# Attention with global and local tokens, then a gated feed-forward layer: the staging of the first two batches rearranged

## The chip, the cores and the metric

The kernel runs on one core of a Trainium2 chip. A core has five engines that each run their own instructions in order: TensorE (PE in the profile: matrix products; PEld its weight loads), VectorE (DVE), ScalarE (ACT), GpSimd (POOL) and SyncE (SP), which here only issues DMAs. They wait for one another through semaphores. Sixteen DMA engines move data between device memory and the on-chip memory (SBUF); TensorE writes only to PSUM, from which VectorE or ScalarE must copy.

The metric is device time in microseconds, the median over several runs of the same program.

## The reference

Eight batches, eight heads, 512 local and 32 global tokens, head width 64. Global queries see all 544 keys; a local query sees the 32 global keys and the local keys within 32 positions. The result goes through a feed-forward layer.

```python
k_all = np.concatenate([k_g, k_l], axis=2)
v_all = np.concatenate([v_g, v_l], axis=2)
out_g = np.matmul(sm(scale * q_g @ k_all.T), v_all)
s_ll = np.where(np.abs(pos[:, None] - pos[None, :]) <= 32, scale * q_l @ k_l.T, -1e9)
s_lg = scale * q_l @ k_g.T
a_l = sm(np.concatenate([s_lg, s_ll], axis=-1))
out_l = np.matmul(a_l, np.concatenate([v_g, v_l], axis=2))
...
h = x @ w_in                       # x: 4352 x 512, w_in: 512 x 2048
g = h * np.clip(h + 3.0, 0.0, 6.0) / 6.0
return (g @ w_out).astype(np.float32)
```

(The transposes are written short.)

## The kernel before

Work is cut into 32 pairs `p` of two heads; a batch `b` has `NM` = 4 pairs. A local pair takes these steps, each a helper:

- `load(p, what)` (L117) issues on SP the DMA of k, q or v, 256 KB of float32 each, into one of 16 staging tiles `stg`. `cast` (L131) makes float16 of it: on GpSimd, but for pair 0's k and q, which VectorE takes. `vshift` (L142) copies half of v into `vb`, whose rows 64 to 95 hold the 32 global values.
- `emit_Tp` (L238) transposes k and q on TensorE; `copy_k` (L249, VectorE) and `copy_q` (L256, ScalarE or VectorE) bring them to SBUF. `emit_T` (L262) does all three and a fourth, small copy at L267: the last 32 queries are repeated in front of the others. For the first four pairs this copy is not made; `emit_Ss` (L313) splits the first window's product in two instead (L319, `p < NM`).
- `emit_S(p, ch)` (L345) and `emit_S4(p)` (L337) compute scores: two matmuls of 512 columns per half `ch` put a mask into PSUM (L310), small matmuls add q times k (L326), ScalarE takes the exponential (L335). Each half has 128 keys; the second holds the 32 global keys beside its local ones.
- `emit_AV(p)` (L370) multiplies by `vt` and `vb` and divides (VectorE, L390 and L391). `emit_X(p)` (L433) transposes the result and copies it to `xt` (VectorE, or ScalarE with `True`).

The global keys go through `load_g`, `cast_G`, `emit_Gp`, `copy_G` (L180 to L213) into `kgT`, and `kglob` or `kglob_m` (L220, L233) repeats them four times in the key tile. The global values are fetched by `load_vg` (L154), a DMA on GpSimd's queue that also casts, and `vglob_m` (L226, VectorE) or `vglob` (L146, GpSimd, later batches) repeats them four times into `vb`. `vgsum` (L151) copies them to `vgs` for the global queries.

The feed-forward layer is cut into units that are put between the steps of attention. `u1(c)` (L467) multiplies four blocks of `w_in` by the four `xt` of the batch into one PSUM tile, 16 values of `c` per batch; ScalarE (L477) and VectorE (L479) make `gt` of it. `u2(t, c4)` (L484) multiplies four `gt` by four blocks of `w_out`. `load_w` and `cast_w` (L159, L168) bring in sixteen blocks of `w_in` and sixteen of `w_out`; `u1(c)` needs blocks 4*(c//4) to 4*(c//4)+3.

The order of every engine is written out by hand: first all loads of batches 0 and 1, the weights and pair 8 (L532 to L563, SP's order), then GpSimd's casts in the same order (L618 to L650), then the steps of TensorE, VectorE and ScalarE (L655 on). The first two batches (pairs 0 to 7) transpose on TensorE; later ones by DMA. From `emit_SG(0)` (L732), the first scores of the global queries, the text of the program is the same in both versions. SP's and ScalarE's DMAs share eight completion semaphores in turn: each DMA waits, in its issuing queue, for the one that had its semaphore before it.

Of the kernel before, what the change touches and what calls it, by code (L numbers as in the profile page):

```python
# [14 lines left out]
def kernel(  # L15
# [12 lines left out]
    nc = tc.nc  # L28
# [4 lines left out]
    dm, dff = moe_w_in.shape  # L33
    NM = H // 2
    NC = dff // P
    NT = Sl // P
# [21 lines left out]
    def const(name, shape, dtype=FP16):  # L58
        return constp.tile(shape, dtype, tag=name, name=name)
# [11 lines left out]
    kgT = const("kgT", [P, NM, B, Sg])  # L71
    vg = const("vg", [P, B, H, D])
    kTs = [const(f"kT{i}", [P, NM, NT * KW + W]) for i in range(2)]
# [4 lines left out]

    NRUN = 2
    NE = 4  # L80
# [65 lines left out]
    def vglob(b, eng):  # L146
        eng.tensor_copy(out=vbs[b % NV][rg, :, :, vc],
                        in_=vg[rg, b].rearrange("s (m h) d -> s m (h d)", h=2).unsqueeze(1)
                        .to_broadcast([Sg, NT, NM, P]))

    def vgsum(b, eng):  # L151
        eng.tensor_copy(out=vgs[b % NV][rg], in_=vg[rg, b])

    def load_vg(b):  # L154
        nc.gpsimd.dma_start(out=vg[rg, b], in_=v_g[b].rearrange("h s d -> s h d"))

# [31 lines left out]
    def cast_G(b0, b1, nm, eng=nc.vector):  # L188
        n = wrk.tile([P, 4 * P], FP16, tag="gn", name=nm + "n", bufs=2)
        nb = b1 - b0  # L190
        eng.tensor_copy(out=n[:, 0:nb * P], in_=gst[b0, nm][:, 0:nb * P])
        gst[b0, nm, "n"] = n
# [12 lines left out]

    def copy_G(b0, b1, nm, x):
        nb = b1 - b0
        kv = (gst[b0, nm, "ps"][x * D:(x + 1) * D, 0:nb * P]
              .rearrange("p (b m e s) -> p e b m s", b=nb, m=MH, e=2))
        for e in range(2):  # L210
            r, ms = slice(e * D, (e + 1) * D), slice(x * MH, (x + 1) * MH)
            o = kgT[r, ms, b0:b1] if nm == "kg" else qgz[r, ms, b0:b1, e]
            nc.vector.tensor_copy(out=o.rearrange("p m b s -> p b m s"), in_=kv[:, e])  # L213

# [10 lines left out]

    def vglob_m(b, ms):  # L226
        n = ms.stop - ms.start
        nc.vector.tensor_copy(
            out=vbs[b % NV][rg, :, ms, vc],
            in_=vg[rg, b].rearrange("s (m h) d -> s m (h d)", h=2)[:, ms].unsqueeze(1)  # L230
            .to_broadcast([Sg, NT, n, P]))

# [29 lines left out]
    def emit_T(p):  # L262
        emit_Tp(p)
        copy_k(p)
        copy_q(p)
        s = st[p]
        nc.scalar.copy(out=s["qT"][:, 0:W].rearrange("p (i j) -> p i j", j=NT),  # L267
                       in_=s["psq"].rearrange("p (j i) -> p i j", j=NT)[:, P - W // NT:P])

# [43 lines left out]
    def emit_Ss(p, ch, exps=True):  # L313
# [4 lines left out]
        for w in range(NT):  # L318
            c0 = w * KW if ch == 0 else ((w - 1) % NT) * KW + D  # L319
            parts = [(w * P, w * P, P)]  # L320
            if w == 0 and p < NM:
                parts = [(0, Sl, W), (W, W, P - W)]
            for o, i, n in parts:
                for e in range(2):
                    r = slice(e * D, (e + 1) * D)
                    nc.tensor.matmul(out=pss[e][:, o:o + n], lhsT=kT[r, c0:c0 + P],  # L326
                                     rhs=qT[r, i:i + n], start=False, stop=True,
                                     skip_group_check=True)
# [16 lines left out]
    def emit_S(p, ch):  # L345
        emit_Sm(p, ch)
        emit_Ss(p, ch)
# [174 lines left out]
    def local_dests(b):  # L522
# [7 lines left out]
        return d  # L530

    load(0, "kq")  # L532
    load(1, "kq")
    load_g(0, 1, "kg")
    load(2, "kq")
    load(0, "v")
    load(3, "kq")
    for p in range(1, NM):
        load(p, "v")
    for i in range(4):  # L540
        load_w("in", i)
    load_g(1, 4, "kg")
    load(4, "kq")
    for i in range(4, 8):
        load_w("in", i)
    load(5, "kq")
    load(4, "v")
    for i in range(8, 12):
        load_w("in", i)
    load(6, "kq")  # L550
    load(5, "v")
    load(7, "kq")
    for i in range(12, NC):
        load_w("in", i)
    load(6, "v")
    load(7, "v")
    load_g(0, 4, "qg")
    for i in range(8):
# [17 lines left out]
    make_identity(nc, ident)  # L576
    load_vg(0)
    mb = const("mb", [P, 2, P])
# [26 lines left out]
    nc.vector.memset(vbs[0], 0.0)  # L605
    ones_v(0, nc.vector)
    mv = mneg.rearrange("p c (w q) -> p c w q", w=NT)
    nc.vector.tensor_copy(out=mv, in_=mb.unsqueeze(2).to_broadcast([P, 2, NT, P]))
# [3 lines left out]
    cast(0, "q", nc.vector)  # L612

    def first(p, what="kqv"):
        cast(p, what, nc.gpsimd)
        vshift(p, nc.gpsimd)

    cast(1, "kq", nc.gpsimd)  # L618
    cast(2, "kq", nc.gpsimd)
    first(0, "v")  # L620
    cast(3, "kq", nc.gpsimd)
    for p in range(1, NM):
        first(p, "v")
    for i in range(4):
        cast_w("in", i, nc.gpsimd)
    cast(4, "kq", nc.gpsimd)
    load_vg(1)
    for i in range(4, 8):
        cast_w("in", i, nc.gpsimd)
    cast(5, "kq", nc.gpsimd)  # L630
    first(4, "v")
    ones_v(1, nc.gpsimd)
    for i in range(8, 12):
        cast_w("in", i, nc.gpsimd)
    cast(6, "kq", nc.gpsimd)
    first(5, "v")
    cast(7, "kq", nc.gpsimd)
    for i in range(12, NC):
        cast_w("in", i, nc.gpsimd)
    first(6, "v")  # L640
    first(7, "v")
    vgsum(0, nc.gpsimd)
    fill_vg(1, nc.gpsimd)
# [9 lines left out]
    lo, hi = slice(0, NM // 2), slice(NM // 2, NM)  # L653
    HEAD = 3
    emit_Tp(0)  # L655
    copy_k(0)
    copy_q(0)
    emit_S(0, 0)
    warm_up(3)
    emit_Tp(1)  # L660
    copy_k(1)
    copy_q(1)
    emit_S(1, 0)
    emit_Gp(0, 1, "kg")
# [8 lines left out]
    emit_S(1, 1)  # L673
    vglob_m(0, lo)
    emit_S(2, 0)
    emit_AV(0)
    vglob_m(0, hi)
    emit_Tp(3)
    copy_k(3)
    copy_q(3)  # L680
    emit_S(2, 1)
    emit_X(0)
    emit_S(3, 0)
    emit_AV(1)
    emit_S(3, 1)
    emit_AV(2)
    emit_X(1)
    emit_X(2, True)
    emit_AV(3)
    for c in range(HEAD):  # L690
        u1(c, range(2))
    emit_X(3)
    for c in range(HEAD):
        u1(c, range(2, 3))
    cast_G(1, 4, "kg")
    for c in range(HEAD):
        u1(c, range(3, 4))
    emit_G(1, 4, "kg")
    u1(3)
    kglob(1, nc.vector)  # L700
    emit_T(4)
    u1(4)
    emit_S4(4)
    emit_T(5)
    vglob_m(1, lo)
    vglob_m(1, hi)
    u1(5)
    emit_S4(5)
    u1(6)
    emit_AV(4)  # L710
    emit_T(6)
    u1(7)
    emit_S4(6)
    emit_X(4)
    emit_AV(5)
    u1(8)
    emit_T(7)
    u1(9)
    emit_S4(7)
    emit_X(5)  # L720
    emit_AV(6)
    for t in Egs:
        nc.vector.memset(t[:, NT], 0.0)
    cast_G(0, 4, "qg")
    u1(10)
    u1(11)
    emit_AV(7)
    emit_X(6)
    emit_G(0, 4, "qg")
    u1(12)  # L730
    u1(13)
    emit_SG(0)  # L732
# [163 lines left out]
```

The softmax here doesn't subtract the row's maximum and nothing guards it: scores larger than these inputs give would overflow.

## Time and profile before

| | us |
|---|---|
| median of 6 runs | 317.72 |
| lowest, highest | 317.27, 318.46 |
| the profiled execution, whole | 317.7 |
| its span in the profile | 315.9 |
| TensorE busy (matmul) | 305.0 |
| VectorE, ScalarE, GpSimd busy | 211.8, 200.3, 153.8 |
| granted TensorE clock, every slice | full |

The profiled execution takes 317.7 us, of which the profile spans 315.9; the 1.8 us between them lie outside what it records. In all views times run from the span's start. A line of the timeline is: start, length, engine, source line, operation, output and input, count, and in brackets the idle time before it and what ended that idle time. A line of the chain of waits is: start, length, what. A matmul's busy time is modelled from its issue to its end; matmuls overlap, so a busy TensorE may still have gaps in its issue. The steady rate is read from rows such as "psH L472 x4" at 0.86 us in the chain: 0.215 us for 512 columns.

### The profile page before, as it was taken

The page shows a single profiled execution, that of the slowest core. Times are in us where ns is not written, and L with a number is a line of the kernel's source. Part 1 is how long each engine was busy: PE and PEld are TensorE (multiplying, and loading weights), DVE is VectorE, ACT ScalarE, POOL GpSimd, SP SyncE. Part 2 cuts the span into 40 slices and gives each one's busy share as a digit, 9 for nine tenths or more (in the row PEclk, how much of TensorE's full clock was granted, in tenths as well). Part 3 has the DMA queues.
Part 4 walks back from the last instruction along what each step waited for, and adds up shares of the span by engine and source line. Part 5 has one row for each costly group of instructions (what it writes and reads, how often), then busy time and mean ns, then how long its engine had stood idle before and what let it go on. Part 6 is the DMA issues. An engine that isn't in the chain of part 4 may idle for free.

```text
span 315.9 us, 7343 instructions
## 1 busy us (share of the span) xinstructions
PE 305.0 (97%) x2688; PEld 162.6 (51%) x2688; DVE 211.8 (67%) x484; ACT 200.3 (63%) x417; POOL 153.8 (49%) x273
## 2 busy tenths in 40 slices
PE   8887899999999999999999999999999999999995
PEld 5453555545555454555555555555555544448444
DVE  5769688896555899579945996468944962489101
ACT  6757877887444994479844994589556941579000
POOL 4777986599856675764674558543411000000000
PEclk9999999999999999999999999999999999999999
DMA  7999999999999999999999899995642002100131
GB/s 208 247 285 326 308 311 246 250 178 226 211 193 249 191 185 189 174 238 189 191 160 172 195 179 204 202 198 107 125 105 86 17 19 83 66 2 1 36 99 66
DMA packets 140260, 53.05 MB, mean 168 GB/s; under 512 B 127552, under 2 KB 131904, under 8 KB 140224
## 3 DMA queue, kind: packets, MB, share of 16 engines
q1 hardware_dynamic: 138048, 52.32, 75.6%
q0 software_dynamic: 2176, 0.26, 2.2%
q8 instruction: 21, 0.34, 0.5%
q14 instruction: 15, 0.12, 0.2%
HBM read 35.13 MB, written 8.91 MB: 139 GB/s over the span
## 4 chain that ended last, share of the span: by engine, by line
PE 79%; DVE 8%; ACT 6%; issue 3%; DMA 2%; SPq 0%; POOL 0%; ACTq 0%
PE po L488 35%; PE psH L472 30%; PE psS L297 3%; DVE gt L479 3%; ACT E L301 2%; PE pav L383 2%; PE pav L386 2%; DVE xn L391 2%; ACT t L477 2%; DMA stg<-in_q_l_dram 2%; PE psSG L357 1%; PE psS L326 1%; ACT E L335 1%; PE po L500 1%; PE pg L423 1%
## 5 line engine op out<-in xcount | busy, mean ns | idle before, releaser
L488 PE MATMUL po<-wout,gt 128*128 128x512 f16 x528 | 122.6, 379 | 0.0
L472 PE MATMUL psH<-xt,win 128*128 128x512 f16 x512 | 119.8, 379 | 2.3 <-DVE gt L479 1.2
L479 DVE SCALAR_TENSOR_TENSOR gt<-t,psH 128x512 f16<-128x512 f32 (+1 forms) x144 | 90.2, 652 | 20.3 <-ACT t L477 19.3
L477 ACT ACTIVATE t<-psH,half_col 128x512 f32<-128x512 f32 (+1 forms) x144 | 92.0, 670 | 18.0 <-PE psH L472 16.5
L472 PEld LDWEIGHTS <-win 128*128 128x128 f16 x576 | 53.3, 98 | 53.8 <-POOL win L174 2.0
L488 PEld LDWEIGHTS <-gt 128*128 128x128 f16 x528 | 48.5, 98 | 52.1
L304 DVE TENSOR_TENSOR E<-E,mk 128x512 f16<-128x512 f16 x96 | 48.1, 533 | 31.5 <-ACT E L301 30.0
L301 ACT ACTIVATE E<-psS 128x512 f16<-128x512 f32 x96 | 49.8, 604 | 13.7 <-PE psS L297 13.6
L492 ACT COPY ot<-po 128x512 f32<-128x512 f32 x16 | 9.4, 586 | 58.7 <-PE po L488 53.1
L140 POOL CAST kn<-stg 128x512 f16<-128x512 f32 x31 | 20.2, 650 | 34.8 <-DMA stg<-in_k_l_dram 34.2
L409 POOL TENSOR_TENSOR s<-Eg 128x128 f32<-128x128 f16 x24 | 10.9, 456 | 33.5 <-ACT Eg L358 32.3
L391 DVE TENSOR_TENSOR xn<-pav,rc 128x256 f16<-128x256 f32 x64 | 26.1, 422 | 1.3
L140 POOL CAST qn<-stg 128x512 f16<-128x512 f32 x31 | 20.4, 657 | 12.2 <-DMA stg<-in_q_l_dram 11.5
L492 DVE COPY ot<-po 128x512 f32<-128x512 f32 x17 | 11.7, 691 | 21.4 <-PE po L488 21.3
L140 POOL CAST vt<-stg 128x512 f16<-128x512 f32 x32 | 20.6, 644 | 8.4 <-DMA stg<-in_v_l_dram 7.8
L144 POOL COPY vb<-vt 64x512 f16<-64x512 f16 x32 | 20.4, 636 | 2.1
L383 PE MATMUL pav<-vt,E 128*128 128x65 f16 x256 | 20.1, 194 | 0.0
L335 ACT ACTIVATE E<-psS 128x512 f16<-128x512 f32 x32 | 16.9, 600 | 4.9 <-PE psS L326 4.9
L386 PE MATMUL pav<-vb,E 128*128 128x65 f16 x256 | 19.9, 195 | 0.0
L383 PEld LDWEIGHTS <-E 128*128 128x128 f16 x256 | 17.9, 99 | 3.4
L386 PEld LDWEIGHTS <-E 128*128 128x128 f16 x256 | 16.8, 97 | 3.2
L297 PEld LDWEIGHTS <-kT 64*128 64x128 f16 x384 | 10.8, 94 | 9.7 <-issue 8.0
(93 smaller groups left out, 276.7 us busy)
## 6 DMA issues: line engine op xcount, KB each, us to landing
stg<-in_k_l_dram SPq DMA_DIRECT2D x32, 256.0 KB, 3.4
stg<-in_q_l_dram SPq DMA_DIRECT2D x32, 256.0 KB, 4.2
stg<-in_v_l_dram SPq DMA_DIRECT2D x32, 256.0 KB, 4.6
out_dram<-ot SPq DMA_DIRECT2D x23, 256.0 KB, 3.7
stg<-in_moe_w_in_dram SPq DMA_DIRECT2D x16, 256.0 KB, 5.9
stg<-in_moe_w_out_dram SPq DMA_DIRECT2D x16, 256.0 KB, 4.6
out_dram<-ot SPq DMA_DIRECT2D x8, 192.0 KB, 3.8
out_dram<-ot SPq DMA_DIRECT2D x16, 64.0 KB, 2.3
```

The costliest lines, as they stand in the source:

```text
L140: eng.tensor_copy(out=o, in_=s[c + "f"])
L144: eng.tensor_copy(out=vbs[b % NV][0:D, :, m, vc], in_=vts[b % NV][D:P, :, m, vc])
L301: nc.scalar.activation(out=E[:, ch, e], in_=pss[2 * ch + e], func=EXP, scale=qk_scale)
L304: nc.vector.tensor_tensor(out=E[:, ch, e], in0=E[:, ch, e], in1=mk[:, ch].rearrange("p w c -> p (w c)"), op=mult)
L383: nc.tensor.matmul(out=o, lhsT=E[:, 0, e, w * P:(w + 1) * P], rhs=vt[:, w, m, c], start=True, stop=False, skip_group_check=True)
L386: nc.tensor.matmul(out=o, lhsT=E[:, 1, e, w * P:(w + 1) * P], rhs=vb[:, (w - 1) % NT, m, c], start=False, stop=True, skip_group_check=True)
L391: nc.vector.tensor_tensor(out=xn[:, 2 * w2:2 * w2 + 2].rearrange("p w (e d) -> p w e d", e=2), in0=po[:, :, 1:1 + P].rearrange("p w (e d) ...
L472: nc.tensor.matmul(out=ps[:, 0:n], lhsT=w_in_t[m][:, c * P:(c + 1) * P], rhs=rhs(m), start=(m == 0), stop=(m == NM - 1), skip_group_check= ...
L477: nc.scalar.activation(out=t1[:, 0:n], in_=ps[:, 0:n], func=RELU, bias=half_col, scale=1.0 / 6.0)
L479: nc.vector.scalar_tensor_tensor(out=gts[c][:, 0:n], in0=t1[:, 0:n], scalar=1.0, in1=ps[:, 0:n], op0=amin, op1=mult)
L488: nc.tensor.matmul(out=po[t][:, 0:dm], lhsT=gts[c][:, t * P:(t + 1) * P], rhs=w_out_t[c // 4][:, c % 4], start=(c == 0), stop=(c == NC - 1))
L492: (nc.scalar.copy if t % 2 else nc.vector.tensor_copy)(out=ot, in_=po[t][:, 0:dm])
```

## The change

Only the part before `emit_SG(0)` changes, and what it loads.

- Global values of batches 0 and 1: no longer fetched by GpSimd's casting DMA and repeated by four VectorE copies. SP loads them as float32 into a staging tile (`load_vgf`), GpSimd casts them into a new tile `vgp` that already holds the ones (`cast_vg`; two new fills on VectorE), and one DMA on ScalarE's queue per batch writes the four repeats (`vglob_dma`).
- Global keys of batches 1 to 3: cast, copied out of PSUM and repeated on ScalarE instead of VectorE (`copy_G(..., nc.scalar.copy)`, `kglob_a`). The cast of the global queries goes from VectorE to GpSimd.
- The small copy at L267 goes for pairs 4 to 7; their first window is split as for pairs 0 to 3.
- Loads and casts: k and q are separate entries; `w_in` blocks stand singly between the k, q and v of later pairs.
- Order of the steps: shown below. `copy_q(3)` moves to VectorE, the copy of `emit_X(1)` to ScalarE, four fills of `Eg` and four of ones to the start of VectorE's list.

```diff
-    NRUN = 2
+    vgp = [const(f"vgp{i}", [P, NM, 2 * DV]) for i in range(NRUN)]
...
-            if w == 0 and p < NM:
+            if w == 0 and p < NRUN * NM:
...
+    def kglob_a(b):
+        kv = kTs[b % 2][:, :, 0:NT * KW].rearrange("p m (u c) -> p m u c", u=NT)
+        nc.scalar.copy(out=kv[:, :, :, P:KW],
+                       in_=kgT[:, :, b].unsqueeze(2).to_broadcast([P, NM, NT, Sg]))
...
+    def load_vgf(b):
+        vgf[b] = stage()[rg].rearrange("s (h d) -> s h d", h=H)
+        nc.sync.dma_start(out=vgf[b], in_=v_g[b].rearrange("h s d -> s h d"))
+
     load(0, "kq")
     load(1, "kq")
     load_g(0, 1, "kg")
-    load(2, "kq")
+    load_vgf(0)
+    load(2, "k")
+    load(2, "q")
     load(0, "v")
...
+    load(1, "v")
+    load_w("in", 0)
+    load(2, "v")
     load_g(1, 4, "kg")
+    load_w("in", 1)
+    load(3, "v")
+    load_w("in", 2)
+    load(4, "k")
+    load_w("in", 3)
+    load(4, "q")
+    load_vgf(1)
+    load_w("in", 4)
...
+    load(7, "k")
+    load_w("in", 12)
+    load(7, "q")
+    load_w("in", 13)
+    load_g(0, 4, "qg")
     load(6, "v")
+    load_w("in", 14)
     load(7, "v")
-    load_g(0, 4, "qg")
+    load_w("in", 15)
...
-    load_vg(0)
...
+    for t in vgp:
+        nc.vector.memset(t[rg], 1.0)
...
+    def cast_vg(b, eng):
+        eng.tensor_copy(out=vgp[b][rg, :, vc], in_=vgf[b].rearrange("s (m h) d -> s m (h d)", h=2))
+
+    def vglob_dma(b):
+        nc.scalar.dma_start(
+            out=vbs[b][rg].rearrange("s u m c -> s u (m c)"),
+            in_=vgp[b][rg].rearrange("s m c -> s (m c)").unsqueeze(1)
+            .to_broadcast([Sg, NT, NM * 2 * DV]))
...
     copy_q(1)
+    vglob_dma(0)
     emit_S(1, 0)
...
     emit_S(1, 1)
-    vglob_m(0, lo)
     emit_S(2, 0)
-    emit_AV(0)
-    vglob_m(0, hi)
     emit_Tp(3)
     copy_k(3)
-    copy_q(3)
+    copy_q(3, True)
+    emit_AV(0)
     emit_S(2, 1)
+    emit_AV(1)
+    emit_S(3, 0)
+    emit_S(3, 1)
     emit_X(0)
-    emit_S(3, 0)
-    emit_AV(1)
-    emit_S(3, 1)
     emit_AV(2)
-    emit_X(1)
+    cast_G(1, 4, "kg", nc.scalar)
+    emit_X(1, True)
+    emit_Gp(1, 4, "kg")
+    for x in range(HH):
+        copy_G(1, 4, "kg", x, nc.scalar.copy)
+    u1s(0)
+    emit_AV(3)
     emit_X(2, True)
-    emit_AV(3)
...
+    kglob_a(1)
+    u1s(1)
     emit_X(3)
...
+    u1s(2)
+    emit_T(4)
+    vglob_dma(1)
+    u1s(3)
+    emit_S4(4)
     u1(3)
...
-    kglob(1, nc.vector)
-    emit_T(4)
+    emit_T(5)
     u1(4)
-    emit_S4(4)
...
```

`u1s(m)` is the m-th quarter of `u1(0)`, `u1(1)` and `u1(2)`. After this the order is: scores 5, AV 4, u1(5), u1(6), T(6), X(4), u1(7), scores 6, T(7), AV 5, u1(8), u1(9), X(5), u1(10), scores 7, AV 6, u1(11), the global queries' transposes, u1(12), X(6), AV 7, u1(13), `emit_SG(0)`.

## Prediction

> **What bounds the kernel now.** I read the page's first two parts, then the busy times by stretches, the chain of waits, and GpSimd's timeline.
>
> ```profile
> span 315.9 us, 7343 instructions
> ...
> PE 305.0 (97%) x2688; PEld 162.6 (51%) x2688; DVE 211.8 (67%) x484; ACT 200.3 (63%) x417; POOL 153.8 (49%) x273
> ...
> PE   8887899999999999999999999999999999999995
> ...
> DMA  7999999999999999999999899995642002100131
> ```
>
> TensorE is full from the seventh slice on; only the first six (7.9 us each) are not. A change before `emit_SG(0)` can only shorten these. The stretches show the room:
>
> ```profile
> 4.60:11.03 6.43, 5.33 (x58) 2.83 (x56) 2.67 (x9) 3.34 (x6) 2.91 (x5) 1.00 1.16 302
> 11.03:20.50 9.47, 8.65 (x157) 5.45 (x154) 7.52 (x22) 7.42 (x14) 7.74 (x14) 1.00 0.96 235
> 20.50:48.10 27.60, 24.31 (x256) 13.54 (x254) 21.42 (x54) 19.53 (x39) 23.54 (x44) 1.00 1.09 316
> ```
>
> Busy time overstates matmul work, so I count it at the chain's steady rates: 0.86 us for an `u1` or a pair's masks, 0.60 for a pair's 16 score matmuls (0.34 for the 10 of a split half), 0.44 for a pair's transposes, 0.50 for an AV, 0.22 for an X. The three stretches then hold 3.6, 7.5 and 23.0 us of work: gaps of 2.8, 2.0 and 4.6 us, 9.4 in all. The third also has the DMA engines at 1.09 and GpSimd at 23.5 of 27.6, so supply may be what limits it.
>
> ```profile
> 2.27 5.32 DMA stg<-in_q_l_dram
> 7.63 0.63 POOL qn L140
> ...
> 48.12 0.45 PE psSG L357 x10
> ...
> 59.86 0.86 PE po L488 x4
> ```
>
> The chain begins with a DMA landing and GpSimd's cast of it. After 48.12 it is nearly all matmul. How regularly loads arrive shows on GpSimd, where a cast waited for DMA:
>
> ```profile
> 6.78 0.61 POOL L140 CAST kn<-stg 128x512 f16<-128x512 f32 x1 [3.59 <-DMA stg<-in_k_l_dram]
> ...
> 34.63 0.62 POOL L140 CAST vt<-stg 128x512 f16<-128x512 f32 x1 [0.21 <-DMA stg<-in_v_l_dram]
> ...
> 36.55 0.61 POOL L140 CAST qn<-stg 128x512 f16<-128x512 f32 x1
> ...
> 40.01 0.62 POOL L140 CAST vt<-stg 128x512 f16<-128x512 f32 x1 [0.42 <-DMA stg<-in_v_l_dram]
> ...
> 57.77 1.34 POOL L174 CAST wout<-stg 128x512 f16<-128x512 f32 x2 [0.27 <-DMA stg<-in_moe_w_out_dram]
> ```
>
> Pair 5's v lands at 34.63, pair 6's at 40.01, seven loads apart: 0.77 us a load. Even the last `w_out` block, at 57.8, makes GpSimd wait. So the load stream is a second bound, close behind TensorE, to about 59 us.
>
> **Part by part.** *The start.* Two new fills (528 values each) stand before VectorE's mask copy. Nearest rows, 0.17 us for 128 words and 0.94 for 1056, give 0.50 each; bounds 0.17 and 0.94. Pair 0's casts follow: k at 4.86 instead of 3.83. TensorE was busy with warm-up until 4.8, so S(0,0) moves only from 6.44 to about 6.8. Against it, `load_vg(0)` goes. Pair 0's q is cast at 4.37 as it lands, pair 1's k at 6.78 as it lands, 2.4 us later, where the next three landings are 0.85, 1.0 and 0.83 us apart; the odd 1.6 us is where that small DMA's packets run. By the same row k1 would land near 5.2. But ScalarE's copy of q1 must wait for pair 0's exponentials (two of 0.54 after S(0,0)): 8.55 instead of 8.74. So S(1,0) gains 0.2 us, not 1.6. The fills of `Eg` and ones (0.5 us together) lie in VectorE's gap of 1.9 us before `copy_k(1)`.
>
> *The repeats of v.* Four VectorE copies of 0.60, 0.47 and twice 0.75 leave: 2.6 us. Two stood ahead of `copy_k(3)`, which ended at 16.29 with TensorE waiting; now it can end at 14.0. Behind them comes a wait: `vglob_dma(0)` stands on ScalarE's queue behind `copy_q(1)` and ahead of the next exponentials, and waits for GpSimd's cast of the global values (done about 7.3) and for pair 2's k (shared semaphore, about 7.4), both before 9.1: no stall. Issue costs ScalarE between nothing and the 0.47 of SP's rows; S(1,0) takes 0.4, so nothing is lost. Its landing no row shows. Bounds: 1.7 us, the median of the 128 KB outputs, and the slowest of GpSimd's small loads, issued into the full stream at 23.2:
>
> ```profile
> DMA to landing us min/median/max: 7.0/7.0/7.0
> ```
>
> I take 4.0, nearest the median of 3.9 of those eight loads. Issued at 9.2 it lands at 13.2; AV(0), now behind `emit_Tp(3)`, stands at 13.45. At 7.0 AV(0) stalls 2.8 us. The second is issued near 23.5 for an AV(4) at 29.2: hidden at either bound.
>
> *Keys on ScalarE.* Cast of 384 columns 0.45 and four copies of 192 columns 0.30 each (between 0.39 for 256 and 0.21 for 32), repeat 0.48, X(1)'s copy 0.48: 2.6 us more on ScalarE, all between the last exponential of pair 3 and the first of pair 4. It loses `copy_q(3)` (0.48) and four L267 copies (0.2 each). VectorE loses 2.0 there (L191, L213, L235).
>
> ```profile
> L258 ACT COPY qT<-psTq x7: 586/586/617, 5.7 to 40.0; 128x512 f16<-128x512 f16 x7
> ...
> L258 DVE COPY qT<-psTq x1: 681/681/681, 12.1 to 12.1; 128x512 f16<-128x512 f16 x1
> ```
>
> These rows say that a copy out of PSUM costs ScalarE no more than VectorE. [...]
>
> *The queues stepped by hand.* Exponentials of pair 3 end at 18.3 (19.2 before). ScalarE's new work, two `xt` copies, q4 and the three `t` (0.6 each) then reach pair 4's exponentials at 25.4, limited by TensorE's masks, where they began at 28.9; pair 5's at 29.2 against 32.0. T(6) comes at 31.5 (33.9), T(7) at 34.6 (39.2). Both are in front of more work now, so T(7) needs q7 early.
>
> *Supply at T(7).* In the new order q7 is the third full load after pair 5's v, behind w11, k7, w12, q7 less the w11 that was already ahead: 34.63 + 3 x 0.77 = 36.95. Minus up to 1.6 for `load_vg(0)`, plus 0.2 for each float32 load of global values (64 KB, a quarter of a load), plus two repeats of 135 KB at 0.45 each by size: 36.65, bounds 35.0 (the repeats nothing, `load_vg(1)` freed too) and 38.3 (nothing freed). The cast takes 0.62, so q7's transposes start at 37.35: TensorE, there at 34.6, waits 2.7 us. An AV(0) stall of up to 2.7 therefore disappears in this wait.
>
> [...] No run here yet shows a DMA of ScalarE's queue. If the repeats were free instead, q7 would come 0.9 us earlier.
>
> From there to `emit_SG(0)`: transposes 0.22, three AV 1.5, six `u1` 5.16, X(5) and X(6) 0.44, scores 7 with the split window 1.56, query transposes 0.22: 9.1 us, so 46.45 against 48.12. Gain 1.65. The 16 added matmuls (0.08 a pair) are in these sums. VectorE's `gt` 11 and four query copies (1.21) end near 46.4 too; in front of SG the old kernel waited 0.76 for the same copies.
>
> *After it.* The second bound takes its share. The `po` at 59.86 needs the last `w_out` block by its fourth matmul, 60.5; the cast ended at 59.11, 1.4 spare. The stream's net change (-1.6 + 0.4 + 0.9) gives 0.3 more: gains over 1.7 are lost there. Nothing later in the chain is a wait for a load, so 1.65 stays: 317.7 - 1.65 = **316.05 us** (span 314.25). The profiled execution and the median, 317.72, agree.
>
> **Rivals.** *More than that (314.7).* If the stream keeps up (q7 by 34.6, `w_out` 1.3 us earlier), the hand-stepped queues reach SG at 45.1: gain 3.0. For it: 1.6 us lost at the start. Against it: the DMA engines are above 1.0 throughout.
>
> *No change (317.6).* The `w_out` casts come no earlier, or 1.2 later, since GpSimd must now pass the last w block (0.62), two global casts and the query cast (1.9 in all, less 0.3 of fills and 1.3 of DMA issue) before them; then everything gained waits at 59.86.
>
> *Slower (319.7): the repeat of batch 1 blocks SP.* `vglob_dma(1)` has w12's semaphore; w12's load on SP may not be issued before it lands, and q7, w13, the global queries and v6 are queued behind. By hand it lands at 27.5 to 30.5, and w12 is due at about 30 (31.4 before). Each us that it lands after 31 delays q7 by as much; from 33.4 SG is later than 48.12. With ScalarE 4 us later than stepped (27.5) and a landing of 7.0 it is 34.5 and q7's transposes start 3.5 us later, 40.9; SG comes at 50.0, 1.9 us later, and 0.1 is lost around it. For: ScalarE must first pass the key copies. Against: 4 us is much.
>
> *It doesn't do what it says*, that is ScalarE stalls where VectorE did: T(7)'s wait covers 2.7 us, so this ends between the first and the second rival.
>
> **How the numbers follow.** About 0.2% (0.64 us) is what a measurement of this kernel can tell from no change. Forecast 0.46, more gain 0.18, no change 0.15, slower 0.21. The forecast and the larger gain are faster by over 0.2%, less 0.02 for the forecast's upper edge, half to each of the others: 0.62; same 0.16; slower 0.22. The forecast's own range, from the bounds of q7's landing (35.0 and 38.3) with the cut at `w_out`, is 315.0 to 317.7. The range that leaves out 2 in 10 goes from 314.5, just past the larger gain, to 318.6, halfway to the slower case.
>
> **What would show it.** Right: pair 1's k cast near 5.2, `copy_k(3)` ended by 14.1, first exponential of pair 4 by 26, T(7) waiting for GpSimd's q7 until about 37, `emit_SG(0)` at 46.4, `po` waiting little before 58.5. Wrong: AV(0) waiting for `vglob_dma(0)` past 16, SP waiting for ScalarE's second DMA, T(7) without a wait, or a gain at SG that is gone at 60.

## The result, and the profile after

The changed kernel takes 319.54 us (median of 20 runs, 318.15 to 322.3), the kernel before 317.70 beside it (41 runs): ratio 1.0061, 95% interval 1.0043 to 1.0079. It is slower by about 1.9 us. The prediction was 316.05, faster. The changed kernel's runs also lie wider apart: in 8 of 21 the mean granted TensorE clock was 0.995 or lower, and the median of these is 1.6 us above that of the others; of 24 runs of the kernel before that went with the first experiments this was so in one.

The profiled execution of the changed kernel took 320.95 us with a span of 319.2, 3.3 us above the span before; that is one execution, 1.4 us above the median, so the shifts read from it are larger than the median's 1.9. First the page's head and its slices (40 of equal length, tenths busy).

```profile
span 319.2 us, 7382 instructions
...
PE   7888889999999999999999999999999999999995
...
DMA  7999989999999999999889998996742002100131
```

TensorE reaches nine tenths from the seventh slice on, before from the sixth. Little is lost behind that: numbered in order, each matmul of `po` from the first to the 40th (53.65 to 79.8 us) starts 3.29 us later than its counterpart before, and the last block 3.5 us later. The loss is made in the opening, so the same three stretches are read again (start:end, length, busy PE, PEld, DVE, ACT, POOL with counts, clock, DMA share, GB/s).

```profile
4.60:11.03 6.43, 5.75 (x47) 3.25 (x46) 3.29 (x18) 2.66 (x5) 3.60 (x6) 1.00 1.08 284
11.03:20.50 9.47, 7.57 (x136) 4.56 (x136) 6.43 (x18) 6.26 (x13) 5.61 (x11) 1.00 1.07 248
20.50:48.10 27.60, 23.20 (x278) 13.43 (x275) 16.73 (x39) 21.47 (x42) 20.88 (x36) 1.00 0.99 276
```

In the third stretch VectorE and GpSimd are less busy than before (16.7 and 20.9 against 21.4 and 23.5 us), TensorE too, and the DMA engines move 276 GB/s where they moved 316. That points to supply, not to an engine. What was waited for stands in the waits from 3 to 52 us (who, for what: us in total, times, longest), and for SyncE's queue from 20 to 50 us:

```profile
PE psTq L247 <- POOL qn L141: 1.8, 1, 1.8
...
PE pav L384 <- DMA vb<-vgp: 1.6, 2, 1.2
...
PE psH L470 <- POOL win L177: 1.3, 1, 1.3
```

```profile
SPq L166 <- DMA vb<-vgp: 2.1, 1, 2.1
```

These are four suspects: pair 7's q comes late, the first value products wait for the first repeat, `u1(4)` waits for w7, and w12's load on SyncE waits for the second repeat to land. The repeats themselves, among the instructions on `vb` from 9 to 27 us:

```profile
L640 ACTq DMA_DIRECT2D vb<-vgp x2: 593/688/782, 9.6 to 25.7; - x2
...
DMA to landing us min/median/max: 6.6/7.2/7.8
```

The issue of each takes 0.59 or 0.78 us of ScalarE's queue, and they land after 6.6 and 7.8 us. The chain of waits names q7 as the long piece just ahead of the end of the opening:

```profile
34.00 6.25 DMA stg<-in_q_l_dram
```

q7 is issued at 34.00 and lands at 40.25 (36.07 before). TensorE's timeline from there on:

```profile
41.04 0.40 PE L247 MATMUL psTq<-ident,qn 128*128 128x128 f16 x4 [1.83 <-POOL qn L141]
...
50.14 0.70 PE L355 MATMUL psSG<-qgz,kT 128*128 128x64 f16 x10
51.23 1.02 PE L470 MATMUL psH<-xt,win 128*128 128x512 f16 x4 [0.40 <-DVE gt L477]
52.12 0.28 PE L442 MATMUL psX<-ident,xn 128*128 128x128 f16 x2
52.66 0.28 PE L442 MATMUL psX<-ident,xn 128*128 128x128 f16 x2 [0.26 <-DVE xn L389]
53.65 0.59 PE L486 MATMUL po<-wout,gt 128*128 128x512 f16 x2
```

and of the kernel before, the same places:

```profile
39.45 0.39 PE L246 MATMUL psTq<-ident,qn 128*128 128x128 f16 x4
...
48.12 0.45 PE L357 MATMUL psSG<-qgz,kT 128*128 128x64 f16 x10 [0.76 <-DVE qgz L213]
48.41 1.03 PE L472 MATMUL psH<-xt,win 128*128 128x512 f16 x4
49.28 0.39 PE L444 MATMUL psX<-ident,xn 128*128 128x128 f16 x4
...
50.36 0.81 PE L488 MATMUL po<-wout,gt 128*128 128x512 f16 x3
```

Three moments hold most of the story: the transposes of q7 (41.04; 39.45 before), the start of `emit_SG(0)` (50.14; 48.12), the first `po` (53.65; 50.36). From the first to the second it is 9.10 us, to the third 3.51 more: 12.61. Before it was 8.67 and 2.24: 10.91. The new order has more work behind q7, and waits for VectorE in it, so it needs q7's transposes 1.7 us earlier than before, at 37.8, only to break even. They come 1.6 us later.

### The profile page after: what moved, and what is told of

Read it like the earlier page. It is cut to its first block, busy times and chain, and to the rows that moved or that the text cites. A ratio compares the mean times of both kernels' runs of the same rounds, so it can differ in the third digit from the quotient of the medians.

```text
span 319.2 us, 7382 instructions
## 1 busy us (share of the span) xinstructions
PE 306.1 (96%) x2704; PEld 163.2 (51%) x2704; DVE 210.1 (66%) x479; ACT 202.0 (63%) x419; POOL 151.8 (48%) x270
## 4 chain that ended last, share of the span: by engine, by line
PE 74%; DMA 8%; DVE 7%; ACT 4%; SPq 3%; issue 2%; POOL 1%; POOLq 0%; ACTq 0%
PE po L486 34%; PE psH L470 28%; DMA stg<-in_moe_w_in_dram 4%; PE psS L295 3%; DVE gt L477 3%; DMA stg<-in_q_l_dram 2%; DMA stg<-in_v_l_dram 2%; SPq L125 2%; PE pav L381 2%; PE pav L384 2%; DVE E L302 2%; ACT E L299 2%; ACT t L475 1%; DVE xn L389 1%; PE psSG L355 1%
## 5 line engine op out<-in xcount | busy, mean ns | idle before, releaser
L302 DVE TENSOR_TENSOR E<-E,mk 128x512 f16<-128x512 f16 x96 | 49.3, 550 | 30.1 <-ACT E L299 28.9
L141 POOL CAST qn<-stg 128x512 f16<-128x512 f32 x31 | 19.7, 635 | 13.1 <-DMA stg<-in_q_l_dram 11.9
L333 ACT ACTIVATE E<-psS 128x512 f16<-128x512 f32 x32 | 16.7, 602 | 6.0 <-PE psS L324 6.0
```

The costliest lines, as they stand in the source:

```text
L141: eng.tensor_copy(out=o, in_=s[c + "f"])
L302: nc.vector.tensor_tensor(out=E[:, ch, e], in0=E[:, ch, e], in1=mk[:, ch].rearrange("p w c -> p (w c)"), op=mult)
```

## The experiments

Every kernel below is timed beside the kernel before on the same chip. T(7) is the start of q7's transposes, SG of `emit_SG(0)`, `po` of the first `po`, each in the one profiled execution; the median is over 6 to 12 runs (before 41, after 20). The profiled execution can lie far from the median (after 1.4 us above it, e2 2.4 above, f3 1.3 below), so what a version is worth is read from the medians; T(7), SG and `po` show only where a time is made.

| kernel | median | ratio to before (95%) | T(7) | SG | po |
|---|---|---|---|---|---|
| before | 317.70 | 1 | 39.45 | 48.12 | 50.36 |
| after | 319.54 | 1.0061 (1.0043 to 1.0079) | 41.04 | 50.14 | 53.65 |
| e1 both repeats on VectorE | 318.21 | 1.0019 (1.0003 to 1.0035) | 37.41 | 46.55 | 50.06 |
| e2 second on VectorE | 319.07 | 1.0056 (1.0030 to 1.0082) | 41.47 | 50.61 | 54.13 |
| e3 first on VectorE | 319.86 | 1.0067 (1.0044 to 1.0091) | 38.56 | 48.37 | 51.22 |
| e4 fills on GpSimd | 319.96 | 1.0090 (1.0060 to 1.0119) | 39.29 | 48.39 | 51.90 |
| e5 w7 earlier | 319.58 | 1.0054 (1.0034 to 1.0074) | 39.54 | 48.63 | 52.14 |
| e6 e1 and w7 earlier | 317.88 | 1.0009 (0.9985 to 1.0033) | 38.21 | 47.34 | 50.85 |
| e7 e6, fills, copies to ScalarE | 318.06 | 1.0002 (0.9983 to 1.0021) | 37.29 | 46.43 | 50.53 |
| e8 e5, second repeat early | 319.78 | 1.0060 (1.0040 to 1.0081) | 40.50 | 49.59 | 53.10 |
| e9 copies in VectorE's gaps | 317.82 | 1.0011 (0.9997 to 1.0025) | 36.80 | 47.32 | 49.83 |
| e10 e9, AV(7) earlier | 317.42 | 0.9999 (0.9981 to 1.0017) | 37.27 | 46.68 | 49.38 |
| e11 e9 and two unread DMAs | 319.50 | 1.0058 (1.0026 to 1.0091) | 40.40 | 49.49 | 53.01 |
| e12 kernel before, repeats by DMA | 319.85 | 1.0075 (1.0055 to 1.0096) | 41.80 | 50.47 | 52.70 |
| f1 e11, a quarter of the bytes | 318.00 | 1.0007 (0.9990 to 1.0023) | 37.02 | 46.12 | 49.63 |
| f2 e11, on 128 rows | 318.42 | 1.0015 (0.9987 to 1.0042) | 38.01 | 47.10 | 50.62 |
| f3 e11, 128 bytes | 318.02 | 1.0011 (0.9993 to 1.0028) | 36.90 | 45.99 | 49.50 |
| f4 e10, kgn cast on VectorE | 317.61 | 0.9983 (0.9955 to 1.0010) | 37.29 | 46.70 | 49.40 |
| g2 e11, every byte read once | 319.36 | 1.0042 (1.0020 to 1.0064) | 38.73 | 47.82 | 51.34 |
| g3 e11, on 64 rows | 319.84 | 1.0070 (1.0045 to 1.0094) | 39.59 | 48.68 | 52.19 |

### One part at a time: the repeats and the fills

e1 sends neither repeat by DMA; e2 and e3 leave out the second or the first alone; e4 moves the fills.

```diff
+    def vglob_v(b, ms):
+        n = ms.stop - ms.start
+        nc.vector.tensor_copy(out=vbs[b][rg, :, ms, vc], in_=vgp[b][rg, ms, vc].unsqueeze(1).to_broadcast([Sg, NT, n, P]))
...
-    vglob_dma(0)
...
     copy_q(3, True)
+    vglob_v(0, lo)
     emit_AV(0)
+    vglob_v(0, hi)
...
-    vglob_dma(1)
...
     emit_T(5)
+    vglob_v(1, lo)
+    vglob_v(1, hi)
```

```diff
     for t in vgp:
-        nc.vector.memset(t[rg], 1.0)
+        nc.gpsimd.memset(t[rg], 1.0)
```

> Both repeats go back to VectorE, as four copies of 0.47 to 0.82 us each by the rows of the kernel before; loads, casts, fills and steps stay those of the changed kernel. Theory A (the repeats' landings, 6.6 and 7.8 us, carry the loss: they hold up the first value products by about 2.8 us and w12 on SyncE's queue by 2.1 us): AV(0) no longer waits for a DMA, w12 is issued near 31.5, q7 near 32.0 instead of 34.0, q7 lands near 38.2, the query transposes of pair 7 start near 39, SG(0) near 48.2, and the median is 317.3 to 318.0, against 319.54 for the changed kernel. Theory B (the order of loads carries it: w7 behind k5, q5 and v4, and q7 and v6 late in the stream whatever SyncE does): SG(0) still starts at 49.5 or later and the median is 319.0 to 319.6. Theory C (the fills on VectorE at the start carry it): as B, and S(0,0) stays near 7.3.

> Only the second batch's repeat goes back to VectorE; the first stays a DMA. Theory A in its narrow form (only the wait of SyncE's queue for the second landing reaches the end): same as with both on VectorE, w12 near 31.5, SG(0) near 48.3, median 317.5 to 318.2. If the first repeat's wait is what reaches the end: SG(0) near 49.5, median 319.0. Theory B: w12 is early but q7 still lands after 39.5, median 319.0 to 319.6.

> Only the first batch's repeat goes back to VectorE; the second stays a DMA. Theory A in its narrow form: AV(0) starts near 14 instead of 16.2, but w12 still waits for the second landing, SG(0) near 50, median 319.2 to 319.7. If the first repeat's wait reaches the end: SG(0) 1 to 2 us earlier, median 318.0 to 318.5. Theory B: 319.0 to 319.6.

> The two fills with ones go to GpSimd; all else stays. Theory C (the start's 0.87 us reach the end): S(0,0) near 6.5, median 318.7 to 319.0. Theories A and B: S(0,0) near 6.5 but q7 lands as before near 40.2, SG(0) within 0.3 of 50.1, median 319.3 to 319.7; GpSimd, which starts its casts after the fills, may add up to 0.5 of its own.

e1 gains 1.3 us in the median; in its profile q7's transposes stand at 37.41 instead of 41.04, SG at 46.55. Its median of 318.21 is just above theory A's upper end. AV(0) still waits 1.6 us, now for VectorE's copies behind `copy_q(3)`. One repeat alone does nothing that shows (e2 319.07, e3 319.86). With e2 the narrow form of A falls: w12 waited for no repeat, and the median is still 319.07. (Its profile, with SG at 50.6, is one of its longest executions; `u1(4)` stood 2.27 us in it waiting for w7.) e4 rejects theory C: S(0,0) starts at 6.45 as expected, and the median stays at 319.96. What the start loses does not reach the end. SG at 48.39 in e4's profile was not expected (50.1).

In e2's profile a fall of the granted clock follows a long wait. TensorE's timeline behind the wait for w7, and the stretches around it:

```profile
32.68 0.61 PE L470 MATMUL psH<-xt,win 128*128 128x512 f16 x1 [2.27 <-POOL win L177]
33.08 1.91 PE L308 MATMUL psS<-mneg,ident 128*128 128x512 f16 x4
34.92 1.04 PE L324 MATMUL psS<-qT,kT 64*128 64x32 f16 x20
```

```profile
30.00:32.00 2.00, 0.39 (x1) 0.10 (x1) 1.56 (x3) 0.85 (x2) 1.44 (x3) 1.00 1.03 331
32.00:34.00 2.00, 1.32 (x4) 0.49 (x5) 0.90 (x2) 0.68 (x1) 2.00 (x4) 0.66 1.11 316
34.00:36.00 2.00, 2.00 (x26) 0.97 (x25) 0.69 (x1) 0.45 (x2) 1.83 (x4) 0.50 1.06 341
```

The granted clock falls to 0.66 and 0.50, and four mask matmuls take 1.91 us instead of 1.03, the scores 1.04 instead of 0.64 (the changed kernel at 31.41 and 32.38): 1.3 us on top of the 2.27.

### The wait for w7, and the semaphore that SyncE shares

e5 swaps w7 and pair 4's v; e6 does so on e1. e8 is e5 with the second repeat sent earlier (the lines shown move up from their later places), so that it has landed before SyncE needs its semaphore. e7 is e6 with the fills on GpSimd and three copies in front of SG on ScalarE.

```diff
-    load(4, "v")
     load_w("in", 7)
+    load(4, "v")
...
-    first(4, "v")
     cast_w("in", 7, nc.gpsimd)
+    first(4, "v")
```

```diff
+    load_vgf(1)
     load_g(1, 4, "kg")
...
     cast_w("in", 0, nc.gpsimd)
+    cast_vg(1, nc.gpsimd)
...
     emit_X(0)
+    vglob_dma(1)
     emit_AV(2)
```

```diff
-    emit_G(0, 4, "qg")
+    emit_Gp(0, 4, "qg")
+    copy_G(0, 4, "qg", 0)
+    copy_G(0, 4, "qg", 1, nc.scalar.copy)
     u1(12)
-    emit_X(6)
+    emit_X(6, True)
```

> The changed kernel with one swap: block 7 of w_in is loaded and cast ahead of pair 4's v instead of behind it (both repeats stay DMAs). u1(4) waited 1.28 us for that block in the profiled run, and up to 2.41 us in the runs so far, where TensorE's granted clock then fell to 0.5 for some 3 us. Theory A (the second repeat blocks SyncE's queue): u1(4) no longer waits, yet w12 still waits for the landing, SG(0) starts at 49.5 to 50.2 and the median is 319.2 to 319.7. Theory D (the wait for w7 costs by itself, and through the clock after it): the runs with a mean clock under 0.998, 8 of 21 so far, become 1 in 10 or fewer, and the median is 318.7 to 319.1. Theory B (the order of loads is the whole loss): SG(0) near 48.3, median 317.7 to 318.2.

> w7 first, and the second repeat stays a DMA of the same bytes but is issued some 5 us earlier (its global values are loaded and cast earlier, the DMA stands on ScalarE's queue behind X(0)), so that it has landed before SyncE needs its semaphore. Read against the kernel with w7 first alone. Lane theory (it is the wait for the landing that costs): SyncE issues w12 near 31, q7 lands near 38, SG(0) near 48 and the median is 0.8 to 1.3 us lower, 318.0 to 318.4. Bytes theory (it is the 132 KB more in a full load stream): q7 still lands after 39, SG(0) within 0.4 us, median within 0.4 us of that kernel's.

> Both repeats on VectorE (that kernel: 318.21, with u1(4) waiting 1.64 us for w7 and SG(0) at 46.55) and w7 ahead of pair 4's v. If w7 is what bounds this version: no wait at u1(4), SG(0) near 45.0 to 45.5, median 316.8 to 317.4. If the gain is lost behind SG(0), where VectorE is full (X(7) and the first po waited there): SG(0) near 45.3 but po at 49.5 or later, median 317.6 to 318.0. If the late loads v6, v7 and w15 bound it: SG(0) unchanged near 46.5, median 318.0 to 318.3.

> As the one before (repeats on VectorE, w7 first), and the fills on GpSimd, and in front of SG(0) half of the global query copies (two of 0.30 us) and X(6)'s copy (0.42) on ScalarE, which waits 0.9 us there. Theory E (VectorE's queue between SG(0) and the first po took 1.3 us of the gain: 3.51 us between them where the kernel before has 2.24): SG(0) to po near 2.4, S(0,0) near 6.5, median 315.6 to 316.4. If SG(0) to po is not VectorE's: that distance stays near 3.5, median 316.8 to 317.4. If w_out's casts, which GpSimd starts near 46.5, decide: po waits for GpSimd, median 317.0 to 317.7.

e5 and e8 decide against the semaphore. In neither profile does SyncE's queue wait for a repeat (the row of 2.1 us is gone), and the medians are 319.58 and 319.78, where the lane theory had 318.0 to 318.4 for e8. The wait of 2.1 us that the profile of the changed kernel shows is real, but the loss is there without it. Theory D fails as well: runs with a lower clock became fewer (2 of 12 against 8 of 21), yet the median did not move. e6 is 0.3 us under e1 and level with the kernel before; `u1(4)` waits no more, but SG comes at 47.34, not at 45.0 to 45.5. e7 gains nothing more: from SG to `po` it takes 4.10 us instead of 3.51, since a matmul waits 0.88 us for the copy that went to ScalarE. So that remedy was wrong, and whether VectorE's order costs was left to e10.

### The transfers with no reader, and the transfers in the old order

e9 puts the VectorE copies where VectorE idles (with fills and w7 as in e7, without its copies on ScalarE). e11 is e9 with both DMAs beside the copies, writing the same shape into rows that nothing reads. e12 is the kernel before with its four copies replaced by the two DMAs; with them come the float32 loads, the fills on GpSimd, and batch 1's ones from GpSimd to VectorE.

```diff
-    vglob_dma(0)
+    vglob_v(0, lo)
...
     copy_q(2, True)
+    vglob_v(0, hi)
...
-    vglob_dma(1)
+    vglob_v(1, lo)
+    vglob_v(1, hi)
```

```diff
     def vglob_dma(b):
         nc.scalar.dma_start(
-            out=vbs[b][rg].rearrange("s u m c -> s u (m c)"),
+            out=vg[b * Sg:(b + 1) * Sg].rearrange("s b h d -> s (b h d)")[:, 0:NT * NM * 2 * DV].rearrange("s (u c) -> s u c", u=NT),
...
     vglob_v(0, lo)
+    vglob_dma(0)
...
+    vglob_dma(1)
     vglob_v(1, lo)
```

```diff
-    load_vg(0)
+    load_vgf(0)
...
     copy_q(1)
+    vglob_dma(0)
...
-    vglob_m(0, lo)
-    vglob_m(0, hi)
...
     emit_T(4)
+    vglob_dma(1)
...
-    vglob_m(1, lo)
-    vglob_m(1, hi)
```

> The changed kernel with the repeats as VectorE copies (0.42 to 0.82 us each) in gaps of VectorE's queue: the first half where the first DMA was issued (VectorE idled 0.98 us there), the second behind copy_q(2) (0.87 us), both of batch 1 where the second DMA was issued; fills on GpSimd; w7 ahead of pair 4's v. In the versions so far the copies stood behind copy_q(3) and AV(0) still waited 1.6 us for them. If the waits of TensorE before 22 us reach the end: AV(0) at 13.5 without a wait, SG(0) near 44.8, first po near 48.5, median 316.2 to 317.0. If the loads or GpSimd's casts set the pace behind it (v6, v7, w15, w_out): the gain is lost there, first po near 50, median 317.4 to 318.0.

> The version with VectorE copies in the gaps, and in addition both DMAs at their old places on ScalarE's queue, of the same shape (32 rows, four times 528 values), into rows that nothing reads: the cost of the transfers without any reader. Bytes theory (two transfers of 132 KB in a full load stream, and what is queued behind them, cost by themselves): 0.9 to 1.7 us above the version without them. Reader theory (only AV(0) and AV(4) waiting for the landing cost): within 0.3 us of it. Lane theory (SyncE waits for a landing whose semaphore it shares): w12 waits in the trace, and 0.5 to 1.5 us above it.

> The kernel before with only its four VectorE copies of the global values replaced by the two DMAs (float32 values loaded behind the first global keys and behind q4, cast on GpSimd, sent where the changed kernel sends them); order of loads, steps and keys as before. If the DMAs are what the change lost by: 318.6 to 319.6 against 317.87, AV(0) waiting for the landing. If they cost only in the new order, where w7 and q7 are due earlier: 317.6 to 318.2. If VectorE's 2.6 us were worth more than the DMAs cost: under 317.4.

e9 and e11 are the pair that settles what the change lost by. Nothing reads what e11's DMAs write, and they cost 319.50 - 317.82 = 1.7 us, nearly as much as the whole change lost (1.8). In the new order the loss is the transfers, not the wait of their readers. GpSimd's casts of two v of batch 0 and TensorE's q7, first e9:

```profile
14.98 0.61 POOL L141 CAST vt<-stg 128x512 f16<-128x512 f32 x1 [0.55 <-DMA stg<-in_v_l_dram]
18.12 0.61 POOL L141 CAST vt<-stg 128x512 f16<-128x512 f32 x1 [1.18 <-DMA stg<-in_v_l_dram]
...
36.80 0.40 PE L247 MATMUL psTq<-ident,qn 128*128 128x128 f16 x4 [0.41 <-POOL qn L141]
```

then e11:

```profile
16.59 0.61 POOL L141 CAST vt<-stg 128x512 f16<-128x512 f32 x1 [1.08 <-DMA stg<-in_v_l_dram]
19.60 0.61 POOL L141 CAST vt<-stg 128x512 f16<-128x512 f32 x1 [1.05 <-DMA stg<-in_v_l_dram]
...
40.40 0.40 PE L247 MATMUL psTq<-ident,qn 128*128 128x128 f16 x4 [1.08 <-POOL qn L141]
```

A cast that waits for its DMA dates the landing. Behind the first transfer the loads land 1.6 and 1.5 us later; by q7, behind both, 3.6 us later.

In e12 the median rises by 2.3 us, past the upper end of what was expected. So the DMAs are dear in the old order too, but there they show in another way: AV(0) waits 2.32 us for the landing, and every landmark behind it is 2.3 us late (q7 41.80, SG 50.47, `po` 52.70), while no matmul between them waits for a load. e12 thus prices a late reader and does not tell it from the transfer itself; e11 does.

e9 lost its lead elsewhere. `u1(12)` waited 1.26 us for w15, which landed at 44.73, and behind the first `po` TensorE waits for GpSimd's casts of `w_out`, one block after another:

```profile
51.57 0.38 PE L486 MATMUL po<-wout,gt 128*128 128x512 f16 x1 [0.18 <-POOL wout L177]
...
52.69 0.38 PE L486 MATMUL po<-wout,gt 128*128 128x512 f16 x1 [0.18 <-POOL wout L177]
```

The first matmul of `po` is 0.53 us earlier than before, the eighth 0.52 later. Here the supply of `w_out`, which the "no change" rival named, does take the gain.

### What of a transfer costs

All on e9 with the two unread DMAs: f1 with a quarter of the bytes, f3 with two values a row, f2 with the 132 KB on 128 rows once, g3 on 64 rows twice, g2 on 32 rows with a source of distinct bytes. The sources, in the order f1, f3, f2, g3, g2 (the destination is shaped to match; f2 and g3 fill all rows of `vgp`; g2's DMAs stand behind the VectorE copies that they read):

```diff
-            in_=vgp[b][rg].rearrange("s m c -> s (m c)").unsqueeze(1).to_broadcast([Sg, NT, NM * 2 * DV]))
+            in_=vgp[b][rg].rearrange("s m c -> s (m c)").unsqueeze(1).to_broadcast([Sg, 1, NM * 2 * DV]))
+            in_=vgp[b][rg].rearrange("s m c -> s (m c)")[:, 0:2])
+            in_=vgp[b].rearrange("s m c -> s (m c)"))
+            in_=vgp[b][0:2 * Sg].rearrange("s m c -> s (m c)").unsqueeze(1).to_broadcast([2 * Sg, 2, NM * 2 * DV]))
+            in_=vbs[b][rg].rearrange("s u m c -> s u (m c)"))
```

> The version with VectorE copies in the gaps (317.82) and the two unread DMAs, each with a quarter of the bytes (32 rows, once 528 values, 33 KB instead of 132). With the full size they cost 1.7 us. If the cost is time on the DMA engines by bytes: a quarter of it, 0.3 to 0.6 us, median 318.1 to 318.4. If it is a cost of one more DMA in the stream (issue on ScalarE of 0.6 to 0.7 us, its semaphore, its turn in the queue): 1.2 to 1.8 us, median 319.0 to 319.6.

> The same with two unread DMAs of 32 rows by 2 values (128 bytes in all), so only the issue and the semaphore are left. Bytes theory: within 0.3 us of 317.82. Issue theory: 0.5 us above it or more.

> The same with two unread DMAs of the full 132 KB, spread over 128 rows of 1056 bytes instead of 32 rows of four times 1056 (all rows of vgp filled). If bytes alone count: 1.4 to 1.9 us as before, median 319.2 to 319.7. If it is the 32 rows (few DMA engines take the load, and later loads wait for the slowest of their sixteen parts): 0.4 to 1.0 us, median 318.2 to 318.8, with the first to last part of a load landing no further apart than without the DMAs.

> The version with VectorE copies in the gaps (317.82) and two unread DMAs of 132 KB on 32 rows again (each row four pieces of 1056 bytes), but the source is the finished copy in vbs, every byte read once, where the change's DMA reads one piece four times; the first is issued behind the second VectorE copy, some 4 us later than before. If reading the same piece again is what made 132 KB cost three times as much on 32 rows as on 128: 0.4 to 0.8 us, median 318.2 to 318.6. If it is the 32 rows: 1.2 to 1.9 us, median 319.0 to 319.7.

> The same with two unread DMAs of 132 KB on 64 rows, each row's piece of 1056 bytes read and written twice. If the number of rows sets the cost (128 rows: 0.6 us, 32 rows: 1.7 us): 0.8 to 1.4 us, median 318.6 to 319.2. If only repeated reading of four times does: nearer to 128 rows, 318.2 to 318.5.

Issue, semaphore and place in the queue cost nothing that shows (in e11 SyncE never waited for one of these DMAs): f3 318.02, f1 318.00, against 317.82 without DMAs. The full bytes on 32 rows cost 1.7 us (e11), read once 1.5 (g2), on 64 rows 2.0 (g3), on 128 rows 0.6 (f2). So it is not the fourfold reading, and not graded by the number of rows, as g3's expectation had it: 64 are as dear as 32. The interval of f2 (0.9987 to 1.0042) lies below that of g3 (1.0045 to 1.0094) and overlaps those of e11 and g2 in part, so that 128 rows are cheaper is shown against 64 rows and likely against 32; T(7) (38.01 against 40.40 in e11) says the same. The 16 landing parts of a load lie about as far apart with the transfers as without them (2.2 and 2.1 us from first to last on average for landings between 5 and 45 us, e11 and e9): the stream as a whole is late. The number of packets is not the difference either: e11, g2, g3 and f2 all send 288 (0.27 MB). By the pages these took 0.4, 0.4, 0.4 and 0.3% of the sixteen engines' span, f1's 0.1%: an estimate from these shares is 1.3 us for the first three, 0.9 for f2 and 0.3 for f1, the order of the costs but not their size.

Why 128 rows are cheaper than 32 or 64 was not isolated here: f2 also moves one piece a row where e11 moves four.

How long a landing takes says little about the bytes. The unread DMAs of 128 bytes (f3), then of 132 KB on 128 rows (f2):

```profile
DMA to landing us min/median/max: 4.6/5.1/5.6
```

```profile
DMA to landing us min/median/max: 5.0/5.7/6.5
```

Even 128 bytes take about 5 us in this full stream; the bytes add 0.6 us on 128 rows, and 1.7 on 32 rows (6.2 to 7.3 in e11).

### Can the rest of the change win?

e10 is e9 with AV(7) ahead of `u1(12)` and X(6); f4 is e10 with the cast of the later global keys back on VectorE.

```diff
     emit_G(0, 4, "qg")
+    emit_AV(7)
     u1(12)
     emit_X(6)
-    emit_AV(7)
     u1(13)
```

```diff
-    cast_G(1, 4, "kg", nc.scalar)
+    cast_G(1, 4, "kg")
```

> As the one before, with AV(7) ahead of u1(12) and X(6) instead of behind them, so that VectorE normalises pair 7 before gt of unit 12 and X(7) does not wait for it. If VectorE's order in front of the first po costs (3.5 us from SG(0) to po against 2.24 in the kernel before): that distance falls to 2.3 to 2.8, median 0.6 to 1.2 us below the version before it. If AV(7) then waits for its exponentials instead: distance down, SG(0) later by as much, median within 0.3 us.

> The version with AV(7) ahead of u1(12) (317.42, repeats by VectorE in its gaps, fills on GpSimd, w7 early), with the cast of the later global keys back on VectorE, since TensorE waited 0.69 us for ScalarE's cast there. If that wait reaches the end: 316.7 to 317.1. If the loads set the pace from there (q7, and w_out behind it): 317.2 to 317.6.

```profile
46.68 0.45 PE L355 MATMUL psSG<-qgz,kT 128*128 128x64 f16 x10
...
48.29 0.39 PE L442 MATMUL psX<-ident,xn 128*128 128x128 f16 x4
...
49.38 1.03 PE L486 MATMUL po<-wout,gt 128*128 128x512 f16 x4
```

In e10 X(7)'s transposes run without a break and SG to `po` is 2.70 us, 0.8 under the 3.51 of the changed kernel: VectorE's order did cost there. The median falls by 0.4 us, less than the expected 0.6 to 1.2, to 317.42. f4 is at 317.61, but it does not take away the wait that it was meant to: TensorE waits 1.30 us for the cast on VectorE where it waited 0.69 for ScalarE's, so whether those 0.69 us reach the end stays open. Both are level with the kernel before (0.9999 and 0.9983, both intervals hold 1), and neither is shown to be faster.

In the profiles of both the first `po` is 1.0 us earlier than before, and at the end 0.4 and 0.1 of it are left. e10 loses 0.3 behind its first `po`. Most of the rest goes at 107 us, in the part that the change doesn't touch, where TensorE waits for a `gt` of VectorE. First the kernel before:

```profile
102.53 1.88 POOL L147 COPY vb<-vg 32x2048 f16<-32x2048 f16 x1
103.45 1.24 DVE L304 TENSOR_TENSOR E<-E,mk 128x512 f16<-128x512 f16 x1 [2.17 <-ACT E L301]
107.09 2.75 PE L472 MATMUL psH<-xt,win 128*128 128x512 f16 x12 [0.41 <-DVE gt L479]
```

then f4:

```profile
102.12 1.88 POOL L148 COPY vb<-vg 32x2048 f16<-32x2048 f16 x1
102.49 1.79 DVE L302 TENSOR_TENSOR E<-E,mk 128x512 f16<-128x512 f16 x1 [2.17 <-ACT E L299]
106.68 2.75 PE L470 MATMUL psH<-xt,win 128*128 128x512 f16 x12 [0.96 <-DVE gt L477]
```

VectorE's product starts 0.96 us earlier in f4 but ends only 0.41 earlier, in both 0.3 us after GpSimd's copy has ended; in the changed kernel, where it starts after that copy (107.05), it takes 0.44. By these rows a gain in front of `emit_SG(0)` can still be lost to this overlap, and e1's last 0.3 us go at the same place; no run moved GpSimd's copy to test it.

## Why the prediction was wrong, step by step

- **The step that failed first: "two repeats of 135 KB at 0.45 each by size".** The 0.45 was an estimate by size; the profile of the kernel before has no DMA on ScalarE's queue to read it from. By size is about right for 128 rows (f2: 0.6 us of the median for both), not for 32. In the profiles the two move q7's transposes by 3.6 us (e9 to e11) where the sum had 0.9, and the median by 1.7. The bounds for q7's landing, 35.0 to 38.3, took the repeats as between nothing and their size, so the range had no room above. Without the repeats T(7) came at 36.8 to 37.4 (e1, e7, e9, e10, f4; 38.2 in e6), where the prediction had 37.35 with them.
- **The second, and the larger in time: "Nothing later in the chain is a wait for a load, so 1.65 stays".** In the changed kernel that is true of loads, and beside the point: the waits behind SG are for VectorE (0.40 for `gt`, 0.26 for `xn`, and slower products of SG). SG to `po` is 3.51 us in the new order, 2.24 in the old: 1.27 lost. e1 shows it alone: SG at 46.55, a gain of 1.57 and as forecast to 0.1 us, of which 0.3 is left at `po` and nothing behind 107 us. Versions that reach `po` earlier wait for `w_out` (e9, e10) or at 107 us (e10, f4).
- "From there to `emit_SG(0)`: 9.1 us" was right: 9.10 in the changed kernel, and 9.09 to 9.14 in thirteen other profiles of the new order; longer only where TensorE waited in between (e3, e9) or where AV(7) was put ahead (e10, f4).
- "I take 4.0" for the landing of a repeat: measured 6.6 and 7.8, the second beyond the upper bound of 7.0. AV(0)'s products with `vb` began at 16.3 instead of 13.45. The median of GpSimd's eight loads was the wrong row; its one load in the full stream, 7.0, was the right one.
- "Hidden at either bound", of the second repeat, is refuted by the trace: TensorE waited 0.41 us at AV(4) and SyncE 2.1 us for w12.
- **The slower rival** (319.7, 0.21) named numbers that came nearly true, q7's transposes at 40.9 (41.04) and SG at 50.0 (50.14), by a mechanism that is not the cause: that these numbers came out is luck. Its wait stands in the trace, but e5 and e8 lose as much without it. The "no change" rival has no part in the changed kernel, as `po` moved as a block, but its `w_out` casts bound e9. ("The DMA engines are above 1.0 throughout" misread the stretches: the second has 0.96. And the page before shows a 9 from the sixth slice on, not the seventh.)
- The start: k of pair 1 was cast at 6.11, not 5.2, and S(0,0) began at 7.31, not 6.8. The fills took 0.52 each (0.50 predicted), and TensorE idled 0.68 us for pair 0's k. e4: no effect on the end.
- A deadline was missed: `u1(4)` needs w7, which the new order puts behind k5, q5 and pair 4's v. It waited 1.28 us. e5, with w7 earlier: no effect on the median.
- Keys on ScalarE were sized right: four copies 1.29 us (1.2 predicted), cast 0.53 (0.45), repeat 0.62 (0.48). That a copy out of PSUM costs ScalarE no more than VectorE holds in the changed kernel for the copies of q (128x512: median 0.59 us against 0.68), not for the key copies (64x192: 0.31 us each; the longest on VectorE before took 0.26). The exponentials of pair 4 began at 28.05, not 25.4, only 0.8 before the old time: ScalarE's copy of q4 waited 1.09 us for TensorE, which had waited 1.18 at AV(0) and 0.7 for the global keys' cast.

In sum: forecast and result lie 3.5 us apart. The rest of the change, forecast at 2.5 us of gain (1.65 and the 0.9 of the repeats), is worth nothing that can be told from the kernel before (e6, e9 and e10: 1.0009, 1.0011, 0.9999); that is the greater part, shown by runs, though which of the waits behind SG takes how much was not isolated. The repeats cost 1.3 (e1) to 1.7 us (e11) of the median instead of 0.9; that is what made the kernel slower and not merely level.

## What to carry to other kernels

In this kernel a transfer beside a full load stream was priced by what it did to the stream, and not by bytes alone: two of 132 KB cost 1.5 to 2.0 us on 32 or 64 rows and 0.6 on 128 (clear against 64 rows, likely against 32). When a step moves, first find the one late arrival that the rest follows from at fixed distance (here q7, then 9.1 and 3.51 us), and compare that distance in both orders before counting what comes earlier; then ask what the unchanged part behind it will wait for once it starts earlier. An experiment that leaves the suspected work in and takes its reader away tells a transfer's own cost from the wait for it.

## What the runs showed of the hardware

- A DMA of 128 bytes on ScalarE's queue landed 4.6 and 5.6 us after its issue while SyncE's loads filled the DMA engines (f3); 132 KB on 32 rows took 5.9 to 7.8 (changed kernel, e11, e12, g2).
- Two such DMAs of 132 KB on 32 rows that nothing reads cost 1.7 us of the median (e11), two of 128 bytes 0.2, less than can be told from none (f3).
- The issue of such a DMA took 0.49 to 0.78 us of ScalarE's queue, more than the 0.47 of SyncE's rows that the prediction had as its bound.
- After TensorE had waited 2.27 us, with 0.39 us of work in the 2 us from 30 to 32, its granted clock was 0.66 from 32 to 34 us and 0.50 from 34 to 36 (e2); after a wait of 2.32 us it was 0.50 from 16 to 19 us (e12, whose mean over the span of 318.0 us was 0.995); a wait of 1.83 us left it at 1.00 (changed kernel, 40 to 42).
- VectorE's product of `E` and the mask took 0.44 us after GpSimd's copy of `vb` had ended (changed kernel) and 1.24 and 1.79 where it began within that copy (before, f4), and ended 0.3 us after it both times.
